# A scaled residual on one core: blocks of 8, 60 and 60 contiguous rows instead of one 128-row block per partition

## The chip, the cores and the metric

The kernel runs on one core of one Trainium2 chip. The metric is the device time in microseconds (us): lower is better. A profile of one execution goes with each kernel. Its span, from the first instruction of the program to the last, is a little shorter than the measured device time.

## The reference

```python
B, S, D = 1024, 16, 512
# x, y: (B, S, D) bfloat16; gamma: (D,) bfloat16
def reference(x, y, gamma):
    return x + gamma * y
```

Seen as a matrix, x and y are 16,384 rows of 512 bfloat16 values, 1 KB a row. The kernel has to read x and y (33.55 MB) and write the result (16.78 MB): 50.33 MB with two arithmetic operations per element.

## The kernel before

Each of the 128 partitions of the on-chip memory (SBUF) gets 128 consecutive rows, so that neighbouring partitions read from places 128 KiB apart in HBM. `SP` and `ACT` list the transfers that the sequencers of SyncE and ScalarE issue, in order, each on a DMA ring of its own: `('y', 4, 64)` loads rows 4 to 64 of every partition, `('x', 64, 117, 0)` does so for x into the buffer rows from 0 on, `('g',)` loads gamma, `('s', 0, 64)` stores. `EARLY` says how many of them are moved ahead of the start-up barrier of the engines.

```python
PIECES = [53, 11, 53, 11]
SP = [('y', 0, 4), ('y', 4, 64), ('x', 0, 64, 0), ('y', 64, 128), ('x', 64, 117, 0), ('x', 117, 128, 64)]
ACT = [('g',), ('s', 0, 64), ('s', 64, 128)]
EARLY = (2, 0)
RELEASE = ('x', 64, 117, 0)
DVE = [('m', 0), ('m', 1), ('a', 0), ('a', 1), ('m', 2), ('m', 3), ('a', 2), ('a', 3)]
# ... (cut)
    xv = xf.rearrange("(p n) d -> p n d", p=P)        # P = 128; the same for yv and ov
# ... (cut)
    y_sb = nc.alloc_sbuf_tensor("y_sb", [P, rows, D], dt).ap()
    x_rows = max(w[3] + w[2] - w[1] for w in x_loads)
    x_sb = nc.alloc_sbuf_tensor("x_sb", [P, x_rows, D], dt).ap()
```

y lies whole in SBUF (128 rows a partition) and the result overwrites it. x has a buffer of 75 rows, parts of which are used twice: a load into rows still in use waits (`frees`) until the additions that read them are done. A store waits for the additions of its rows, and the first one also for `s_go`.

VectorE works through `DVE`: `('m', c)` multiplies piece c of y by gamma, in place, and `('a', c)` adds x to it. `PIECES` has the rows of each piece.

```python
    _take(s_load[RELEASE], 16, nc.tensor)   # when the transfer RELEASE has landed ...
    nc.tensor.sem_inc(s_go, 1)              # ... the stores may start
    nc.tensor.sem_inc(s_rel, 1)
# ... (cut)
    for kind, *args in DVE:
        c = args[0]
        yt = y_sb[:, starts[c] : starts[c + 1], :]
        if kind == "m":
            need(y_loads, c)                # wait for the loads of these rows
            g = gamma_sb[:, None, :].to_broadcast([P, PIECES[c], D])
            nc.vector.tensor_tensor(out=yt, in0=yt, in1=g, op=MULT).then_inc(s_dve, 1)
        else:
            need(x_loads, c)
            # ... (cut)
            nc.vector.tensor_tensor(out=yt, in0=xt, in1=yt, op=ADD).then_inc(s_add, 1)
```

gamma itself is one row; a matmul with a row of ones spreads it over the 128 partitions, and VectorE copies it from there to SBUF.

Of the kernel before, what the change touches and what calls it, by code (L numbers as in the profile page):

```python
# [3 lines left out]


PIECES = [53, 11, 53, 11]

SP = [('y', 0, 4), ('y', 4, 64), ('x', 0, 64, 0), ('y', 64, 128), ('x', 64, 117, 0), ('x', 117, 128, 64)]  # L10
ACT = [('g',), ('s', 0, 64), ('s', 64, 128)]

EARLY = (2, 0)


RELEASE = ('x', 64, 117, 0)

DVE = [('m', 0), ('m', 1), ('a', 0), ('a', 1), ('m', 2), ('m', 3), ('a', 2), ('a', 3)]
MULT, ADD = mybir.AluOpType.mult, mybir.AluOpType.add


def _take(sem, n, eng):


    return eng.wait_ge(sem, n).then_inc(sem, -n)  # L25


def kernel(
# [10 lines left out]
    P = nc.NUM_PARTITIONS  # L39
# [3 lines left out]
    xf = x.flatten_outer_dims()  # L43
    yf = y.flatten_outer_dims()
    of = out.flatten_outer_dims()
    N, D = xf.shape
    rows = N // P
    n = len(PIECES)
    assert sum(PIECES) == rows
    starts = [sum(PIECES[:c]) for c in range(n + 1)]  # L50
    dt = xf.dtype
    xv = xf.rearrange("(p n) d -> p n d", p=P)
    yv = yf.rearrange("(p n) d -> p n d", p=P)
    ov = of.rearrange("(p n) d -> p n d", p=P)

    gamma_row = nc.alloc_sbuf_tensor("gamma_row", [1, D], dt).ap()
    ones_row = nc.alloc_sbuf_tensor("ones_row", [1, P], dt).ap()
# [1 line left out]
    y_sb = nc.alloc_sbuf_tensor("y_sb", [P, rows, D], dt).ap()  # L59
    x_loads = [w for w in SP + ACT if w[0] == "x"]  # L60
    y_loads = [w for w in SP + ACT if w[0] == "y"]
    stores = [w for w in SP + ACT if w[0] == "s"]
    for loads in (x_loads, y_loads, stores):
# [7 lines left out]
    s_load = {w: sem("s_" + "_".join(map(str, w[:2]))) for w in x_loads + y_loads}  # L71
    s_add, s_go, s_rel, s_end, s_out = sem("s_add"), sem("s_go"), sem("s_rel"), sem("s_end"), sem("s_out")
    added = [a for kind, *a in DVE if kind == "a"]
    order = {a[0]: k for k, a in enumerate(added)}

    def meets(a, b, c, d):
        return a < d and c < b

    def pieces_of(a, b):
        return [c for c in range(n) if meets(starts[c], starts[c + 1], a, b)]  # L80

    def x_at(row):
        return next(w[3] + row - w[1] for w in x_loads if w[1] <= row < w[2])

    def frees(w):

        c = set()
        for v in x_loads[: x_loads.index(w)]:
            lo, hi = max(v[3], w[3]), min(v[3] + v[2] - v[1], w[3] + w[2] - w[1])
            if lo < hi:  # L90
                c |= set(pieces_of(v[1] + lo - v[3], v[1] + hi - v[3]))
        return sorted(c)
# [3 lines left out]
    def ring(eng, what, n_early):  # L96

        known, went = 0, False
        for k, w in enumerate(what):
            kind = w[0]  # L100
            need = frees(w) if kind == "x" else pieces_of(w[1], w[2]) + list(w[3:]) if kind == "s" else []
            need = max((order[c] + 1 for c in need), default=0)
            if kind == "s" and not went:
                _take(s_go, 1, eng)
                went = True
            if need > known:
                eng.wait_ge(s_add, need)
                known = need
            if kind == "g":
                i = eng.dma_start(out=gamma_row, in_=gamma.unsqueeze(0)).then_inc(s_gamma, 16)  # L110
            elif kind == "x":
                to = x_sb[:, w[3] : w[3] + w[2] - w[1], :]
                i = eng.dma_start(out=to, in_=xv[:, w[1] : w[2], :]).then_inc(s_load[w], 16)
            elif kind == "y":
                r = slice(w[1], w[2])
                i = eng.dma_start(out=y_sb[:, r, :], in_=yv[:, r, :]).then_inc(s_load[w], 16)
            else:
                r = slice(w[1], w[2])
                i = eng.dma_start(out=ov[:, r, :], in_=y_sb[:, r, :]).then_inc(s_out, 16)
            if k < n_early:  # L120
                early.append(i.ins)

    ring(nc.sync, SP, EARLY[0])
    ring(nc.scalar, ACT, EARLY[1])


# [7 lines left out]

    _take(s_load[RELEASE], 16, nc.tensor)
    nc.tensor.sem_inc(s_go, 1)
# [4 lines left out]
    def need(loads, c):  # L141
        for w in loads:
            if w not in landed and meets(starts[c], starts[c + 1], w[1], w[2]):
                if w == RELEASE:
                    _take(s_rel, 1, nc.vector)
                else:
                    _take(s_load[w], 16, nc.vector)
                landed.add(w)
# [5 lines that stand above are left out]
            need(y_loads, c)  # L154
            g = gamma_sb[:, None, :].to_broadcast([P, PIECES[c], D])
            nc.vector.tensor_tensor(out=yt, in0=yt, in1=g, op=MULT).then_inc(s_dve, 1)  # L156
            open_mults += 1
        else:
# [4 lines left out]
            at = x_at(starts[c])  # L163
            xt = x_sb[:, at : at + PIECES[c], :]
            nc.vector.tensor_tensor(out=yt, in0=xt, in1=yt, op=ADD).then_inc(s_add, 1)  # L165
# [44 lines left out]
```

## Time and profile before

| | before |
|---|---|
| device time, median of 3 runs | 119.94 us (119.78 to 120.6) |
| span of the profiled execution | 118.7 us |
| VectorE busy | 70.0 us, 59% of the span |
| TensorE matmul busy | 0.6 us |
| DMA, both rings | 50.33 MB in 1154 packets, mean 424 GB/s |

How to read it: the page gives the busy time of each engine and cuts the span into 40 slices, in each of which a digit is the busy share in tenths. A DMA transfer is cut into packets, here one for each partition, that 16 DMA engines work on. The queue called q1 is SyncE's ring and q10 ScalarE's. A packet is booked where it starts, so that a slice or a window with a row of long packets starting in it can show more than the engines' whole time, and the next one nothing. A DMA issue is listed with its size and the time from issue to landing, which includes the time that it stood behind others.

### The profile page before, as it was taken

The numbers are of one execution on the slowest core, as the hardware profiler recorded it, in microseconds if no ns is written. First come the engines' busy times: TensorE is split into PE (matmuls) and PEld (weight loads), VectorE is DVE, ScalarE is ACT, GpSimd is POOL, SyncE is SP. The second block draws the span as 40 slices with busy tenths as digits, with TensorE's granted clock in tenths as the row PEclk, the third lists the DMA queues.
The fourth block names the chain that finished last, engine by engine and source line by source line (L and its number), as shares of the span: only waits on it lengthen the run. The fifth ranks groups of instructions, "written<-read, shape, count | busy, mean of one in ns | idle before, by whom it ended". The sixth has DMA issues, their size and how long they took to land. (4 is left out here: it accounts for less than half of the span.)

```text
span 118.7 us, 80 instructions
## 1 busy us (share of the span) xinstructions
PE 0.6 (0%) x1; PEld 0.1 (0%) x1; DVE 70.0 (59%) x10; POOL 0.2 (0%) x4
## 2 busy tenths in 40 slices
PE   0001000000000000000000000000000000000000
PEld 0000000000000000000000000000000000000000
DVE  0002000599999299999759999999999910000000
POOL 0000000000000000000000000000000000000000
DMA  8977977998899888998896969498899889988891
GB/s 268 571 332 331 663 331 331 596 464 353 353 486 574 353 353 353 640 420 353 353 585 293 585 293 585 205 634 353 353 596 464 353 353 420 640 353 353 353 663 44
DMA packets 1154, 50.33 MB, mean 424 GB/s; under 512 B 129, under 2 KB 130, under 8 KB 258
## 3 DMA queue, kind: packets, MB, share of 16 engines
q1 hardware_dynamic: 864, 33.55, 66.0%
q10 hardware_dynamic: 290, 16.78, 32.6%
HBM read 33.56 MB, written 16.78 MB: 424 GB/s over the span
## 5 line engine op out<-in xcount | busy, mean ns | idle before, releaser
L156 DVE TENSOR_TENSOR y_sb<-y_sb,gamma_sb 128x27136 bf16<-128x27136 bf16 (+1 forms) x4 | 34.6, 8688 | 12.3 <-DVEq L25 12.3
L165 DVE TENSOR_TENSOR y_sb<-x_sb,y_sb 128x27136 bf16<-128x27136 bf16 (+1 forms) x4 | 34.6, 8689 | 2.3 <-DVEq L25 2.2
L132 DVE CAST gamma_sb<-gamma_ps 128x512 bf16<-128x512 f32 x1 | 0.7, 692 | 8.8 <-DVEq L25 8.8
L127 DVE MEMSET ones_row<- 1x128 bf16 x1 | 0.2, 165 | 2.0 <-PEq L41 2.0
L130 PE MATMUL gamma_ps<-gamma_row,ones_row 1*128 1x512 bf16 x1 | 0.6, 577 | 10.2 <-PEq L25 10.2
L130 PEld LDWEIGHTS gamma_ps<-gamma_row,ones_row 1*128 1x128 bf16 x1 | 0.1, 99 | 10.2 <-issue 10.2
L194 POOL MEMSET const-bfloat16-1.0<- 128x1 bf16 x1 | 0.1, 101 | 0.0
L194 POOL MEMSET const-uint8-127<- 128x1 uint8 x1 | 0.1, 101 | 0.0
L194 POOL MEMSET const-float32-0.0<- 128x1 f32 x1 | 0.1, 98 | 0.2 <-issue 0.2
L194 POOL MEMSET const-float32-1.0<- 128x1 f32 x1 | 0.1, 98 | 0.0
## 6 DMA issues: line engine op xcount, KB each, us to landing
y_sb<-in_y_dram SPq DMA_DIRECT2D x1, 7680.0 KB, 21.4
x_sb<-in_x_dram SPq DMA_DIRECT2D x1, 6784.0 KB, 20.8
x_sb<-in_x_dram SPq DMA_DIRECT2D x1, 1408.0 KB, 23.8
y_sb<-in_y_dram SPq DMA_DIRECT2D x1, 512.0 KB, 3.8
out_dram<-y_sb ACTq DMA_DIRECT2D x2, 22.8
x_sb<-in_x_dram SPq DMA_DIRECT2D x1, 39.3
gamma_row<-in_gamma_dram ACTq DMA_DIRECT2D x1, 1.0 KB
y_sb<-in_y_dram SPq DMA_DIRECT2D x1, 58.3
```

What stands on the lines that cost most here:

```text
L127: nc.vector.memset(ones_row, 1.0).then_inc(s_ones, 1)
L130: nc.tensor.matmul(gamma_ps, ones_row, gamma_row, start=True, stop=True).then_inc(s_ps, 1)
L132: nc.vector.tensor_copy(out=gamma_sb, in_=gamma_ps).then_inc(s_dve, 1)
L156: nc.vector.tensor_tensor(out=yt, in0=yt, in1=g, op=MULT).then_inc(s_dve, 1)
L165: nc.vector.tensor_tensor(out=yt, in0=xt, in1=yt, op=ADD).then_inc(s_add, 1)
L194: nc = _bacc.Bacc("TRN2", target_bir_lowering=False, num_devices=1)
```

## The change

The rows are cut into three blocks, the first with 8 rows for each partition and the other two with 60; within a block the rows of all partitions lie together in HBM, so that a partition's 8 (or 60) rows are next to those of its neighbours. The first 8 rows of y come as two transfers of 4 rows, one on each ring, both ahead of the start-up barrier. The first 8 rows of x are loaded last of all loads, behind the transfer that releases the stores, and their result is stored last. The pieces and the order of VectorE's work follow from this: in the middle block the last 45 rows are added first, since the next load of x overwrites their place.

The aim is that the first transfers set all DMA engines to work at once, on addresses that lie close together, that small pieces stand at the start and at the end of the work, and that x's 8 rows keep the engines busy between the release of the stores and their first packets.

```diff
-PIECES = [53, 11, 53, 11]
-SP = [('y', 0, 4), ('y', 4, 64), ('x', 0, 64, 0), ('y', 64, 128), ('x', 64, 117, 0), ('x', 117, 128, 64)]
-ACT = [('g',), ('s', 0, 64), ('s', 64, 128)]
-EARLY = (2, 0)
-RELEASE = ('x', 64, 117, 0)
-DVE = [('m', 0), ('m', 1), ('a', 0), ('a', 1), ('m', 2), ('m', 3), ('a', 2), ('a', 3)]
+BLOCKS = [8, 60, 60]
+PIECES = [8, 15, 45, 60]
+SP = [
+    ('y', 0, 4),
+    ('y', 8, 68),
+    ('x', 8, 68, 0),
+    ('y', 68, 128),
+    ('x', 68, 128, 15),
+    ('x', 0, 8, 0),
+]
+ACT = [('y', 4, 8), ('g',), ('s', 8, 68), ('s', 68, 128), ('s', 0, 8)]
+EARLY = (2, 1)
+RELEASE = ('x', 68, 128, 15)
+DVE = [('m', 0), ('m', 1), ('m', 2), ('a', 2), ('a', 1), ('m', 3), ('a', 3), ('a', 0)]
...
-    xv = xf.rearrange("(p n) d -> p n d", p=P)
...
+    def rows_of(t, a, b):
+        c = max(c for c in range(len(BLOCKS)) if edges[c] <= a)
+        assert b <= edges[c + 1]
+        block = t[P * edges[c] : P * edges[c + 1]].rearrange("(p n) d -> p n d", p=P)
+        return block[:, a - edges[c] : b - edges[c], :]
...
-                i = eng.dma_start(out=to, in_=xv[:, w[1] : w[2], :]).then_inc(s_load[w], 16)
+                i = eng.dma_start(out=to, in_=rows_of(xf, w[1], w[2])).then_inc(s_load[w], 16)
```

(The loads of y and the stores are changed in the same way.)

More of the change, by code (lines that the diff above doesn't have):

```diff
@@ L51 @@
     dt = xf.dtype
-    xv = xf.rearrange("(p n) d -> p n d", p=P)
-    yv = yf.rearrange("(p n) d -> p n d", p=P)
-    ov = of.rearrange("(p n) d -> p n d", p=P)
+    edges = [sum(BLOCKS[:c]) for c in range(len(BLOCKS) + 1)]
+    assert edges[-1] == rows
+    def rows_of(t, a, b):
[3 more added lines that the diff above has]
+        return block[:, a - edges[c] : b - edges[c], :]
     gamma_row = nc.alloc_sbuf_tensor("gamma_row", [1, D], dt).ap()
@@ L112, in ring @@
                 to = x_sb[:, w[3] : w[3] + w[2] - w[1], :]
-                i = eng.dma_start(out=to, in_=xv[:, w[1] : w[2], :]).then_inc(s_load[w], 16)
+                i = eng.dma_start(out=to, in_=rows_of(xf, w[1], w[2])).then_inc(s_load[w], 16)
             elif kind == "y":
                 r = slice(w[1], w[2])
-                i = eng.dma_start(out=y_sb[:, r, :], in_=yv[:, r, :]).then_inc(s_load[w], 16)
+                i = eng.dma_start(out=y_sb[:, r, :], in_=rows_of(yf, w[1], w[2])).then_inc(s_load[w], 16)
             else:
                 r = slice(w[1], w[2])
-                i = eng.dma_start(out=ov[:, r, :], in_=y_sb[:, r, :]).then_inc(s_out, 16)
+                i = eng.dma_start(out=rows_of(of, w[1], w[2]), in_=y_sb[:, r, :]).then_inc(s_out, 16)
             if k < n_early:
```

## The prediction

> **What bounds the kernel now.** I read the page first (busy shares, then the slices, then the queues), then the DMA view for sizes and landings, then the timeline and the waits of VectorE, and last the DMA view of narrow windows, to get the time of one packet. The page:
>
> ```profile
> DVE  0002000599999299999759999999999910000000
> ...
> DMA  8977977998899888998896969498899889988891
> ...
> DMA packets 1154, 50.33 MB, mean 424 GB/s; under 512 B 129, under 2 KB 130, under 8 KB 258
> ## 3 DMA queue, kind: packets, MB, share of 16 engines
> q1 hardware_dynamic: 864, 33.55, 66.0%
> q10 hardware_dynamic: 290, 16.78, 32.6%
> ```
>
> Together the two queues keep the 16 DMA engines busy for 66.0 + 32.6 = 98.6% of the 118.7 us span, or 117.0 us per engine; VectorE has 70.0 us in all and ends at 95.4 us. So this is a kernel that moves 50.33 MB and hides everything else. The chain of waits is of little use here: it names 10.4% of "issue" and one VectorE add, because what is waited for is a transfer.
>
> The DMA view of four short windows gives the time of a packet (16 packets, one per engine, start in the last two; the share is their whole duration over 16 engines x the window). Windows 1.0 to 1.5, 2.0 to 2.5, 5 to 6 and 115 to 116 us:
>
> ```profile
> q1 hardware_dynamic: 16, 0.07, 138.4%
> ...
> q1 hardware_dynamic: 46, 0.19, 98.6%
> ...
> q1 hardware_dynamic: 16, 0.98, 226.7%
> ...
> q10 hardware_dynamic: 16, 1.05, 241.8%
> ```
>
> - 5 to 6 us: 60-row packets, 61,440 B each, 2.267 us. That is 27.1 GB/s per engine, 434 GB/s for 16.
> - 115 to 116 us: the stores' 65,536 B packets take 2.418 us, the same rate. They are the last; the span ends at 118.7.
> - 1.0 to 1.5 us: the first 16 packets of 4,096 B. 138.4% x 16 x 0.5 / 16 = 0.69 us each.
> - 2.0 to 2.5 us: the same kind of packet takes 0.986 x 16 x 0.5 / 46 = 0.17 us (0.159 in nearly all single records).
>
> So only the start is slow. The window 1.4 to 2.0 us has 17 packet starts, where 16 engines at 0.159 us could start 60. After that no engine stands still: the landings of the loads, issue time plus time to landing, follow at the packet rate. The lines for them and the timeline of VectorE:
>
> ```profile
> y_sb<-in_y_dram SPq DMA_DIRECT2D x1, 7680.0 KB, 21.4
> x_sb<-in_x_dram SPq DMA_DIRECT2D x1, 6784.0 KB, 20.8
> x_sb<-in_x_dram SPq DMA_DIRECT2D x1, 1408.0 KB, 23.8
> y_sb<-in_y_dram SPq DMA_DIRECT2D x1, 512.0 KB, 3.8
> ...
> y_sb<-in_y_dram SPq DMA_DIRECT2D x1, 58.3
> ```
>
> ```profile
> 10.97 0.69 DVE L132 CAST gamma_sb<-gamma_ps 128x512 bf16<-128x512 f32 x1 [8.81 <-DVEq L25]
> 21.99 17.29 DVE L156 TENSOR_TENSOR y_sb<-y_sb,gamma_sb 128x27136 bf16<-128x27136 bf16 x2 [10.33 <-DVEq L25]
> 41.46 17.29 DVE L165 TENSOR_TENSOR y_sb<-x_sb,y_sb 128x27136 bf16<-128x27136 bf16 x2 [2.17 <-DVEq L25]
> 60.69 17.29 DVE L156 TENSOR_TENSOR y_sb<-y_sb,gamma_sb 128x27136 bf16<-128x27136 bf16 x2 [1.94 <-DVEq L25]
> 78.13 17.30 DVE L165 TENSOR_TENSOR y_sb<-x_sb,y_sb 128x27136 bf16<-128x27136 bf16 x2
> ```
>
> y's first 4 rows land at 3.8 us, its next 60 at 21.9 (18.1 later; 8 packets x 2.267 = 18.1), x's 64 at 41.2, y's 64 at 60.6, x's 53 at 76.6 and 11 at 79.9; the second store is issued at 95.5, some 3 us before the engines have finished the first.
>
> **What the Trainium skill says.** "DMA: Bandwidth & Descriptors", section "Where 436 GB/s comes from", gives a ceiling of 435.2 GB/s; the 434 above agrees, so no layout in HBM can speed up the steady part. Its section "Latency and other measured facts" lists row pitches of 512 KiB (207 GB/s per direction) to 8 MiB (103) for HBM copies, the large ones slow. Here the pitch between partitions is 128 rows x 1 KB = 128 KiB and the rate is full, so there is nothing of that to mend in mid-stream. Its section "Queues, rings and completion order" says that each engine goes round robin between queues by packet. The trace shows what it means for a small transfer: gamma, issued at 1.91 us on ScalarE's ring, has its 1 KB packet only in the window 7 to 8 us and its semaphore packet in 9 to 10, between 61,440 B packets of the other ring. "Issuing engines are not separate DMA queues" says that a second ring saves issue time alone.
>
> **The change part by part.** Everything is worked per engine, because each has a fixed 8 of the 128 partitions and 8 packets of every transfer, and the slowest sets the end.
>
> 1. *Bytes:* the same 50.33 MB. At 61,440 B per 2.267 us, 3.146 MB per engine are 116.1 us, in both kernels.
> 2. *Packets.* 8 packets x durations. Before: 0.159 (4 rows) + 2.267 (60) + 2.418 x 2 (x and y 64) + 2.004 (53) + 0.422 (11) + 2.418 x 2 (stores) = 14.52, x 8 = 116.2 us. After: 0.159 x 2 + 2.267 x 4 loads + 2.267 x 2 stores + 0.310 x 2 (x's 8 rows in and out) = 14.54, x 8 = 116.3. The 0.310 is an estimate from 0.159 at 4 KB and 0.422 at 11 KB. The smaller packets cost 0.1 us.
> 3. *Start.* Packet work of 116.2 in a span of 118.7 leaves 2.5 us: 1.0 from issue to the first packet, about 0.35 from the last engine's last packet to the end (semaphores), and about 1.1 of ramp and spread between engines. The ramp is the 0.69 against 0.159 us of the first packet (0.5), then the empty stretch until the second (a few tenths). The change works on this in two ways. The second ring puts another 4 KB packet in front of each engine in that stretch: at most one or two packets of 0.159 us, 0.15 to 0.3. The rows of 1 MB in one block, instead of 128 places 128 KiB apart, may shorten the first access; nothing in this trace shows it, so I count 0 to 0.3.
> 4. *VectorE.* It is as busy as before: 14.291 us / 53 rows = 0.270 us a row, so 256 row-steps are 69 us. Expected order: y's 8 rows landed by about 5 us, gamma somewhere at 8 to 15 (now behind y's 4 rows on its ring), multiply of 8 rows 2.2 us, done before y 8:68 lands at about 22.9. Multiplies of 15 and 45 rows until 39.2; x 8:68 lands at 41.1; add of 45 rows until 53.4, add of 15 until 57.5. Multiply of 60: 59.3 to 75.6; x 68:128 lands at 77.3; add of 60 until 93.6; add of 8 until 95.8.
> 5. *Reloads.* x 68:128 needs only the 45-row add, so it is issued at 53.4 instead of 55.8; the engines run out of y at about 58.9 (landing 59.3 less 0.35). Issue to first packet took 1.0 at the start, so 4 us are spare. x's 8 rows wait until 57.5, with 18 us of x 68:128 still ahead of them.
> 6. *Stores.* Released by x 68:128 at 77.3 + 0.35. From there to packets was at most 2 us before. x's 8 rows now cover 8 x 0.31 = 2.5 us of it where 11 rows covered 3.4. The fastest engine may stand still for a tenth or two; the slowest is 0.6 behind and does not. Second store: issued at 93.6, engines busy with the first until about 97.5. Third at 95.8, queued far ahead.
>
> Sum: +0.1 for packets, -0.2 to -0.5 for the ramp, 0 for the rest: about -0.3 us. 119.94 - 0.3 = 119.6 us. The unit of the gain is the ramp, and all of it is 1.1 us, 0.9%.
>
> **The rivals.**
> - *The rings start at different moments.* If ScalarE's 4 rows come behind even a few of SyncE's 4 KB packets, the leftover ones each wait out a 2.267 us packet, as gamma did: y's rows 4 to 8 then land at 10 to 20 us and gamma after them. The bytes still flow, and VectorE has until about 22.9 - 2.2 = 20.7. For it: gamma's delay; against: ScalarE's first instruction in this trace is at 0.13 us, as early as SyncE's. Time unchanged to +0.3 only if gamma passes 25 us, as the slack behind it is 2 us at x 8:68 and 4 at the reload.
> - *A gap at the turn from loads to stores,* if 2.5 us of cover are too few. Against it: in the trace the stores' first packets follow the 11-row packets on every engine without a gap. If the store's lead is really above 2.5 us: +0.2 to +0.6, 120.2.
> - *Contiguity is worth more than I count.* If the ramp vanishes and the engines finish together: -1.0, 118.9. A full rate of 434 in mid-stream forbids more.
> - *Spread:* the end is the slowest engine's; 0.64 us lie between the first and the last engine's final packet in the window 117.6 to 118.7. With two rings it may shrink or grow by some tenths.
>
> **Range and chances.** The terms have a width of about 0.4 us each way and the three runs before spread from 119.78 to 120.6; hence 119.6, with 119.1 to 120.2 for 8 in 10. Two per cent is 2.4 us. A gain of that size would need the whole ramp and a rate above the ceiling; a loss of that size needs a hole in the transfers that none of the slacks (4 us and 4 us) suggests. So 0.02 faster, 0.95 within 2%, 0.03 slower.
>
> **What would show it.** Right: 16-packet windows of 2.267 us throughout, a queue share still at 98 to 99%, the first x reload issued near 53.4, the first store near 77.6, and the 60-row packets starting before 4.3 us on all engines (y's 1 MB at full rate needs 2.6 from 1.0, plus ramp). Step 3 is wrong if the first packets of both rings take the same 0.7 us with the same empty stretch, step 6 if slices near 78 to 80 us fall under the mean. All of it is wrong if packets of the new layout take longer than 2.267 us.

## The result, and the profile after

The changed kernel takes 120.75 us (median of 5 runs, 120.69 to 120.8) against 119.89 us (119.78 to 120.6): 1.0067 times the time before, with a 95% interval of 1.0047 to 1.0088. It is slower by 0.7%, and outside the predicted range. The spans of the two profiled executions differ by 0.7 us (119.4 and 118.7).

The page of the changed kernel: the slices and the queues.

```profile
DVE  0004500099999489999589999559999950000000
...
DMA  5999889979979979979989989697997997897796
...
DMA packets 1442, 50.33 MB, mean 421 GB/s; under 512 B 161, under 2 KB 162, under 8 KB 418
## 3 DMA queue, kind: packets, MB, share of 16 engines
q1 hardware_dynamic: 864, 33.03, 64.6%
q10 hardware_dynamic: 578, 17.30, 33.6%
```

The bytes are the same and the engines are as busy as before, 64.6 + 33.6 = 98.2% of the span. The one slice that stands out is the first, the first 3 us: 5 tenths, where the page before has 8. The DMA view of the window 12 to 20 us shows that the 60-row packets are as they were:

```profile
q1 hardware_dynamic: 49, 3.01, 86.8%
```

86.8% x 16 x 8 us / 49 packets = 2.267 us, to the last digit the time of a 61,440 B packet before. So it is the start. The same view in the windows 1.0 to 1.5, 1.5 to 2.0, 2.0 to 2.5 and 2.5 to 3.0 us (in the last one, two queues):

```profile
q1 hardware_dynamic: 21, 0.09, 53.9%
...
q1 hardware_dynamic: 29, 0.12, 84.0%
...
q1 hardware_dynamic: 29, 0.12, 99.7%
...
q1 hardware_dynamic: 21, 0.09, 82.1%
q10 hardware_dynamic: 7, 0.03, 13.9%
```

These are 4 KB packets. In the first window they take 53.9% x 8 us / 21 = 0.21 us each, where the kernel before needed 0.69: the first access did get shorter. But then they get slower, 84.0% x 8 / 29 = 0.23, 99.7% x 8 / 29 = 0.275 and 82.1% x 8 / 21 = 0.31 us, where the kernel before had 0.17 at 2.0 to 2.5 us, 46 packets in half a microsecond instead of 29. And engines stand empty: the packets of the first window fill at most 53.9% of the engines' time. In the packet records of the trace (start, duration and size of every packet) eight packets are under way from 1.3 to 1.7 us, for 16 engines; the kernel before has 14. The change was to set all engines to work at once, and here did the opposite. ScalarE's ring, q10, has no packet at all until the last of these windows; its first one starts at 2.77 us. Its packets take 0.159 us.

The packet records give the sum. The slowest engine starts its first 60-row packet at 5.255 us (before: 3.384). That is 1.87 later, and 8 more packets of 0.159 explain 1.27; 0.60 us are lost. From there to the last packet of the slowest engine it is 118.979 - 5.255 = 113.72 us (before: 118.336 - 3.384 = 114.95), 1.23 less; since 1.27 of the work has moved ahead, 0.04 is lost. The end after the last packet has 0.45 instead of 0.37 us. 0.60 + 0.04 + 0.08 = 0.72, the difference of the spans. The further 0.14 us between the two device times is in no view; other executions of the kernel before with a span of 118.7 us took about 120.0 us, so that most of it is spread between executions.

What the 0.60 us consist of can be worked out too. Per engine, the 4 KB packets ahead of the 60-row ones take 0.72 us more than 0.159 each (before: 0.64, of which 0.53 in the first). From 1.0 us to its first 60-row packet, an engine is without a packet for 0.44 us (before: 0.18). And the slowest engine is 0.55 us behind the mean (before: 0.29): eight engines start their first 60-row packet at 4.29 to 4.45 us, the other eight at 4.94 to 5.26. So longer packets alone give 0.08 of the 0.60, because the shorter first access pays for most of them; gaps and unevenness give 0.26 each.

The timeline after, for the order of the rest:

```profile
0.00 0.84 SPq L130 DMA_DIRECT2D y_sb<-in_y_dram  x2
0.12 0.38 ACTq L130 DMA_DIRECT2D y_sb<-in_y_dram  x1
...
54.40 4.40 SPq L127 DMA_DIRECT2D x_sb<-in_x_dram  x2
60.24 16.16 DVE L170 TENSOR_TENSOR y_sb<-y_sb,gamma_sb 128x30720 bf16<-128x30720 bf16 x1 [1.80 <-DVEq L33]
78.60 19.02 ACTq L133 DMA_DIRECT2D out_dram<-y_sb  x3
78.89 18.36 DVE L179 TENSOR_TENSOR y_sb<-x_sb,y_sb 128x30720 bf16<-128x30720 bf16 x2 [2.49 <-DVEq L33]
```

The second ring's transfer is issued 0.12 us after the first, so the late q10 packets are not a late issue. Reloads and stores are issued in the expected order, each 0.9 to 1.5 us later than expected, and VectorE still waits for the transfers.

### The profile page after: what moved, and what is told of

It is laid out like the page before. It is cut to its first block, busy times and chain, and to the rows that moved or that the text cites. A ratio compares the mean times of both kernels' runs of the same rounds, so it can differ in the third digit from the quotient of the medians.

```text
span 119.4 us, 83 instructions
## 1 busy us (share of the span) xinstructions
PE 0.6 (0%) x1; PEld 0.1 (0%) x1; DVE 70.1 (59%) x10; POOL 0.2 (0%) x4
## 3 DMA queue, kind: packets, MB, share of 16 engines
q1 hardware_dynamic: 864, 33.03, 64.6%
q10 hardware_dynamic: 578, 17.30, 33.6%
## 5 line engine op out<-in xcount | busy, mean ns | idle before, releaser
L170 DVE TENSOR_TENSOR y_sb<-y_sb,gamma_sb 128x4096 bf16<-128x4096 bf16 (+3 forms) x4 | 34.7, 8690 | 12.6 <-DVEq L33 12.6
L179 DVE TENSOR_TENSOR y_sb<-x_sb,y_sb 128x23040 bf16<-128x23040 bf16 (+3 forms) x4 | 34.6, 8686 | 4.5 <-DVEq L33 4.5
```

## The experiments

Each kernel was timed beside the kernel before on the same chip, so that the ratios compare the groups and the times do so only roughly; that one had medians of 120.02, 120.05, 120.02 and 120.06 us in the four groups below. "Start loss" is worked out from the packet records: the start of the slowest engine's first packet of 60 (in one run 64) rows, less the 1.0 us to the first packet and the packets ahead of it at 0.159 us for 4 KB (16 or 8 of them) or 0.309 us for 8 KB (8 of them). The kernel before has 3.38 - 1.0 - 1.27 = 1.11 us, the changed one 5.255 - 1.0 - 2.544 = 1.71. It is that of the one profiled execution; those of e6_pitch16 (121.02 us) and e12_pitch32 (120.41) were 0.2 and 0.4 us above their medians.

### First group: the ring, the layout, the number of packets

```diff
 # e1_one_ring, against the changed kernel
-    ('y', 0, 4), ('y', 8, 68),
+    ('y', 0, 4), ('y', 4, 8), ('y', 8, 68),
-ACT = [('y', 4, 8), ('g',), ...
+ACT = [('g',), ...
-EARLY = (2, 1)
+EARLY = (3, 0)
 # e2_wide_two_rings
-BLOCKS = [8, 60, 60]
+BLOCKS = [128]
 # e3_wide_one_ring: both of the above
 # e4_one_transfer
-    ('y', 0, 4), ('y', 8, 68),
+    ('y', 0, 8), ('y', 8, 68),
-ACT = [('y', 4, 8), ('g',), ...
+ACT = [('g',), ...
-EARLY = (2, 1)
+EARLY = (2, 0)
```

> The changed kernel, but all of y's first 8 rows on SyncE's ring: two transfers of 4 rows, one behind the other, then the 60 rows. Theory A (the contiguous addresses of the first rows slow its 4 KB packets, 0.248 us on average against 0.159): the ring does not matter, 120.7 us, the slowest engine still starts its 60-row packets near 5.2 us. Theory B (the second ring is what slows the start: two transfers are set up side by side): back to about 120.0 us, 60-row packets from 4.6 us at the latest. Theory C (16 small packets per engine at the start instead of 8 cost it, wherever they come from): 120.7 us.

> The changed kernel with its order and both rings, but the rows laid out as before, 128 consecutive rows a partition. Theory A: the 4 KB packets of the start take 0.16 us again after their first, about 119.9 to 120.1 us. Theory B: 120.7 us. Theory C: 120.7 us.

> Layout of before and one ring for y's first rows, with the pieces and the order of the changed kernel. Theory A: as with two rings in this layout, 119.9 to 120.1 us. Theory B: 120.0 us. Theory C: still 120.7 us, as the 16 small packets are there. If all of it comes from the start, this one is within 0.2 us of the kernel before under A and B.

> The changed kernel with y's first 8 rows as one transfer of 8 KB packets on SyncE's ring. Theory A: the packets are contiguous over the whole 1 MB, still slow for a start of the same length: 120.4 to 120.7 us. Theory B: 120.0 us. Theory C: half of the small packets are gone, 120.2 us.

| kernel | us | ratio to before (95%) | start loss, us |
|---|---|---|---|
| e1_one_ring | 120.79 | 1.0065 (1.0053 to 1.0077) | 1.76 |
| e2_wide_two_rings | 120.04 | 1.0001 (0.9994 to 1.0009) | 1.08 |
| e3_wide_one_ring | 120.1 | 1.0005 (0.9997 to 1.0013) | 1.08 |
| e4_one_transfer | 119.87 | 0.9989 (0.9981 to 0.9996) | 0.86 |

The ring does nothing in either layout, so theory B falls. The layout does everything, with all 16 small packets in place: theory C falls too. The DMA view of e2_wide_two_rings, 2.0 to 2.5 us, has the line of before again, 46 packets at 1.012 x 8 / 46 = 0.18 us:

```profile
q1 hardware_dynamic: 46, 0.19, 101.2%
```

Theory A had the three first runs right and missed the fourth: one 8 KB transfer of the same 1 MB is fast. In its view from 1.5 to 2.5 us 40 packets of 8 KB start, 0.33 MB where the changed kernel has 0.24 MB in 58:

```profile
q1 hardware_dynamic: 40, 0.33, 81.7%
```

So it is not that the rows lie close together. What differs between the two, besides the size and number of the packets, is that a 4-row transfer takes 4 KB and leaves out the next 4 KB, through the whole block. In the packet records it has eight packets under way until 1.55 us, like the changed kernel, but then all engines start their 60-row packets within 0.25 us: eight engines that start late are not a loss by themselves. This kernel is also a little faster than both kernels of the case.

### Second group: the distance between the places that are read, and the second ring's late start

```diff
 # e5_pitch4, e6_pitch16: y's two first transfers alone
-    in_=rows_of(yf, w[1], w[2])
+    in_=src
 #  e5:  src = yf[128 * w[1] : 128 * w[2]].rearrange("(p n) d -> p n d", p=P)
 #  e6:  src = yf[0 : 16 * P].rearrange("(p n) d -> p n d", p=P)[:, r, :]
 # e7_scalar_first
-EARLY = (2, 1)
+EARLY = (0, 1)
 # e8_before_no_small, against the kernel before
-SP = [('y', 0, 4), ('y', 4, 64), ('x', 0, 64, 0), ...
+SP = [('y', 0, 64), ('x', 0, 64, 0), ...
-EARLY = (2, 0)
+EARLY = (1, 0)
```

In e5 and e6 (and in e12 to e14 below), y's first 8 rows of each partition are other rows of y than the reference asks for; the work is the same.

> The changed kernel, but y's first two transfers read 4 KB a partition from places 4 KB apart: each is one closed block of 512 KB. Other rows of y than the reference wants come to these places; bytes, packets, rings and order are those of the changed kernel. Theory A1 (a transfer that takes 4 KB and leaves 4 KB out, over 1 MB, uses only a part of what serves these addresses): the 4 KB packets are back to 0.16 us, the time near 120.1 us. Theory A2 (4 KB packets from any small stretch of HBM are slow, since all 16 engines read it at once): as slow or slower, 120.7 us or more, packets of 0.25 us or more.

> As the run before, with places 16 KB apart: 4 KB read, 12 KB left out, over 2 MB. A1: a quarter of these addresses is used at a time, slower than the changed kernel, 121 us or more, packets of 0.4 us. A2: a longer stretch is better, 120.2 to 120.6 us. With places 128 KB apart the packets took 0.159 us, so if this one is fast too, only the 8 KB pitch is bad.

> The changed kernel, with SyncE's two first transfers put back behind the start-up barrier, so that ScalarE's 4 rows of y are the only early transfer. In the changed kernel ScalarE issues them at 0.12 us and their first packet starts at 2.77. Theory S (transfers of both rings are set up one after the other): here the first packet comes 1.0 us after the issue. Theory L (ScalarE's ring is slow to begin): again 2.5 us or more after the issue.

> The kernel before, with y's rows 0 to 64 as one first transfer instead of 4 and 60 rows. If small packets at the start only add their 0.008 us each and the slow first access is paid once whatever its size, 119.8 to 119.95 us, as with one 8 KB transfer in the changed kernel. If a small first transfer does something for the start, 120.2 us or more.

| kernel | us | ratio to before (95%) | start loss, us |
|---|---|---|---|
| e5_pitch4 | 119.78 | 0.9981 (0.9974 to 0.9988) | 0.76 |
| e6_pitch16 | 120.81 | 1.0065 (1.0049 to 1.008) | 1.89 |
| e7_scalar_first | 122.49 (one run) | | |
| e8_before_no_small | 119.98 | 0.9996 (0.9987 to 1.0004) | |

e5_pitch4 is the sharpest run of all: against the changed kernel nothing is different but 4 KB from every 4 KB instead of 4 KB from every 8 (and so which rows come), and 0.97 us are gone. It is the two-ring start as it was meant to be. Its DMA view from 1.5 to 2.5 us, both queues:

```profile
q1 hardware_dynamic: 89, 0.36, 97.8%
q10 hardware_dynamic: 3, 0.01, 5.2%
```

92 packets at 1.03 x 16 / 92 = 0.18 us, against 58 at 0.25 us in the changed kernel, whose line for this window is

```profile
q1 hardware_dynamic: 58, 0.24, 91.9%
```

Theory A2 falls. A1 has e5 right in kind (it said 120.1), but not e6: with a quarter in use the loss is barely larger than with a half, 1.89 us against 1.71, and the packets do not take 0.4 us on average. The same view of e6_pitch16, 0.863 x 16 / 45 = 0.31 us:

```profile
q1 hardware_dynamic: 45, 0.18, 86.3%
```

e7_scalar_first answers for the ring. Its timeline and the window 1.0 to 1.5 us:

```profile
0.13 0.38 ACTq L130 DMA_DIRECT2D y_sb<-in_y_dram  x1
```

```profile
q10 hardware_dynamic: 15, 0.06, 35.5%
```

Alone, ScalarE's transfer has its first packet at 1.14 us, 1.01 after the issue; behind SyncE's it took 2.65. So ScalarE's ring is not slow to begin, and theory L falls. Theory S fits: the second ring's packets came late because the first ring's were ahead of them (in the changed kernel 91 of SyncE's 128 had started by 2.77 us), and could not fill the empty moment after the first packets. How the transfers are set up is in no trace. (The time of 122.49 us only says that a late start on SyncE costs what it delays.) The run shows something else as well: SyncE's rows 0 to 4, here the second transfer over the same block, are slow too. In the window 3.5 to 4.5 us, where 60 of the 63 packets are of 4 KB and the others write semaphores, 0.972 x 16 / 60 = 0.26 us:

```profile
q1 hardware_dynamic: 63, 0.25, 97.2%
```

e8_before_no_small lies just above its forecast of 119.8 to 119.95 and is not distinguishable from the kernel before: leaving out the small first transfer neither helps nor hurts.

### Third group: elsewhere in the work, versions that are right for the reference, and 32 KB

```diff
 # e9_split_late, against e4_one_transfer
-    ('x', 0, 8, 0),
+    ('x', 0, 4, 0), ('x', 4, 8, 4),
 # e10_two_closed, against the changed kernel
-BLOCKS = [8, 60, 60]
+BLOCKS = [4, 4, 60, 60]
-    ('x', 0, 8, 0),                 # and ('s', 0, 8)
+    ('x', 0, 4, 0), ('x', 4, 8, 4), # and ('s', 0, 4), ('s', 4, 8)
 # e11_one_closed4
+BLOCKS = [4, 64, 60]
+PIECES = [4, 15, 49, 60]
+SP = [('y', 0, 4), ('y', 4, 68), ('x', 4, 68, 0), ('y', 68, 128),
+      ('x', 68, 122, 15), ('x', 122, 128, 69), ('x', 0, 4, 0)]
+ACT = [('g',), ('s', 4, 68), ('s', 68, 128), ('s', 0, 4)]
+EARLY = (2, 0)
+RELEASE = ('x', 68, 122, 15)
 # e12_pitch32: as e6_pitch16, with 32 in place of 16
```

> The kernel with y's 8 rows as one transfer (119.87 us), in which x's 8 rows now come as two transfers of 4 rows, 4 KB read and 4 KB left out, in the middle of the work. Theory P (the half-used stretch is slow wherever it stands in the work): these packets take 0.25 us and the slowest engine loses 0.6, about 120.4 us. Theory W (only at the start, where nothing of these addresses was touched and the queues are empty): packets of 0.159 us, 119.9 to 120.0 us.

> The changed kernel with its first block cut into two blocks of 4 rows, so that each of y's two first transfers reads a closed 512 KB, and every row goes where the reference wants it; x's and the result's 8 rows come in two transfers each. Theory A1: 4 KB packets of 0.159 us after the first; 119.8 to 119.95 us, since the four more 4-row transfers cost about 0.1 us against the same start with 8-row transfers (119.78).

> Blocks of 4, 64 and 60 rows: a single closed 4-row transfer of y first, on SyncE's ring; the stores released by x's rows 68 to 122, with 6 and 4 rows of x behind them. Fewest small packets with a closed start: A1 expects 119.65 to 119.8 us, faster than the kernel before (120.0) and than the changed one. If the gain of the closed start needs two rings, 119.9 us.

> The changed kernel with y's first 4-row transfers reading 4 KB from places 32 KB apart (other rows of y than the reference wants). Places 8 and 16 KB apart gave 120.7 to 120.8, 4 KB 119.78 and 128 KB 120.04. If what counts is the share of a stretch that is used, 120.8 or more; if it is the length of the stretch (4 MB here), between 120.0 and 120.5 us.

| kernel | us | ratio to before (95%) | start loss, us |
|---|---|---|---|
| e9_split_late | 120.37 | 1.0028 (1.0017 to 1.004) | 0.95 |
| e10_two_closed | 119.86 | 0.9991 (0.9983 to 0.9999) | 0.74 |
| e11_one_closed4 | 119.94 | 0.9988 (0.9981 to 0.9994) | 0.60 |
| e12_pitch32 | 120.02 | 0.9999 (0.999 to 1.0008) | 1.15 |

e9_split_late shows that the pattern is slow in mid-stream too. x's 4-row transfer, in the middle of a busy ring, from 77.2 to 77.7 us:

```profile
q1 hardware_dynamic: 39, 0.16, 120.0%
```

1.2 x 8 / 39 = 0.25 us for 4 KB. In the kernel without the split (e4_one_transfer, 77.5 to 78.0 us) 8 KB take 1.044 x 8 / 27 = 0.31:

```profile
q1 hardware_dynamic: 27, 0.22, 104.4%
```

The split costs 120.37 - 119.87 = 0.5 us. In the packet records the loss is in the first of the two 4-row transfers, whose packets reach 0.40 us; the second transfer of x takes 0.159 us in all of them. It is not the splitting as such: e10_two_closed has two 4-row transfers of x in the same place, each from a closed block, and their 256 packets take 0.159 us on average and none over 0.17. Why the second pass over such a block is fast here and in the changed kernel, but not in e7_scalar_first, remains open.

e10_two_closed and e11_one_closed4 compute what the reference asks for and, like e4_one_transfer, are faster than the kernel before by about 0.1%, with intervals that just exclude 1; with so many runs side by side that is weak. e11 missed its forecast of 119.65 to 119.8: it starts best of all (0.60), but the first 64-row packets behind it take up to 2.68 us instead of 2.42, so a part of the loss may have moved on to them. e12_pitch32 contradicts the reading that only the share counts: an eighth of 4 MB is in use, and it is as fast as 128 KB. Its forecast for a reading by the length of the stretch, 120.0 to 120.5 us, is met. Its line for 1.5 to 2.5 us, 0.736 x 16 / 68 = 0.17 us:

```profile
q1 hardware_dynamic: 68, 0.28, 73.6%
```

### Fourth group: powers of two, or any part

```diff
 # e13_pitch12, e14_pitch24: as e6_pitch16, with 12 and 24 in place of 16
```

> The changed kernel with y's first 4-row transfers reading 4 KB from places 12 KB apart (other rows of y than the reference wants). Theory U (any small stretch that is used in part is slow): a third of 1.5 MB is used at a time, between 8 KB (120.7) and 16 KB (120.8), so 120.7 us. Theory Z (only distances that are powers of two, 8 and 16 KB, make the 16 engines meet; the odd multiple 3 x 4 KB does not): 119.8 to 120.1 us, and the packets at 1.5 to 2.5 us take 0.16 to 0.18.

> As the run before, with places 24 KB apart, 3 x 8 KB, over 3 MB. Theory U, with the stretch beginning to be long enough (32 KB apart gave 120.02): 120.2 to 120.6 us. Theory Z: 24 KB is a multiple of 8 KB, but not a power of two; 119.8 to 120.1 us, or, if the factor of 8 KB is what counts, as slow as 8 KB, 120.7.

| places apart | 4 KB | 8 KB | 12 KB | 16 KB | 24 KB | 32 KB | 128 KB |
|---|---|---|---|---|---|---|---|
| us | 119.78 | 120.75 | 120.13 | 120.81 | 120.41 | 120.02 | 120.04 |
| start loss, us | 0.76 | 1.71 | 1.13 | 1.89 | 1.44 | 1.15 | 1.08 |
| of it: packets over 0.159 | 0.20 | 0.72 | 0.72 | 0.64 | 0.69 | 0.49 | 0.62 |
| engine without a packet | 0.26 | 0.44 | 0.15 | 0.59 | 0.25 | 0.28 | 0.13 |
| slowest engine behind the mean | 0.29 | 0.55 | 0.27 | 0.67 | 0.49 | 0.38 | 0.33 |

The 8 KB column is the changed kernel, the 128 KB column e2_wide_two_rings, where all transfers have this distance; in the others only y's two first ones have the distance named. The three parts are worked out from the packet records, per engine and up to the first 60-row packet, and rounded.

e13_pitch12 is at 1.0013 (1.0006 to 1.002) and e14_pitch24 at 1.0037 (1.0023 to 1.0052). The window 1.5 to 2.5 us of e13_pitch12, 0.631 x 16 / 53 = 0.19 us:

```profile
q1 hardware_dynamic: 53, 0.22, 63.1%
```

That of e14_pitch24, 0.726 x 16 / 47 = 0.25 us:

```profile
q1 hardware_dynamic: 47, 0.19, 72.6%
```

12 KB uses less of its stretch than 8 KB and is fast, so theory U falls: being used in part is not enough. (Its forecast for 24 KB, 120.2 to 120.6 us, was met, but by an allowance for the length of the stretch.) Theory Z comes close at 12 KB (120.13 against its 119.8 to 120.1; 0.19 against 0.16 to 0.18 us), but at 24 KB it offered either a fast start or one as slow as 8 KB, and the run lies between. So 4 and 12 KB are fast, 8 and 16 KB slow, 24 KB half as bad, 32 and 128 KB fast. That looks like engines meeting at the same places of the memory, by the distance of what they read at the same time; this is argued from the pattern, not shown, and no run here looks at the memory itself.

The parts in the table warn against a simpler story. At 12 and 128 KB the packets together take as long as at 8 and 16 KB: their first ones are slow (0.65 and 0.63 us on average for the first 16), the later ones fast. What 8 and 16 KB have more of is time without a packet and distance between the engines. Only at 4 KB are the packets themselves clearly shorter.

## Why the prediction was wrong, by its own steps

**The bound, and step 1 (bytes):** right. The engines stay 98% busy and the 60-row packets take 2.267 us.

**Step 2 (packets):** right. It put +0.1 us on the smaller packets. In the packet records all packets take 117.24 us per engine instead of 117.01; without the 0.07 of it at the start, 0.16 more.

**Step 3 (start): here it failed**, in both of its terms; the 1.1 us that it put on ramp and spread before are confirmed (1.11). "The second ring puts another 4 KB packet in front of each engine in that stretch": the second ring's first packet started at 2.77 us, when that stretch was over, behind the first ring's (alone it comes 1.01 us after its issue, e7_scalar_first); and taking the ring away changes nothing (e1_one_ring, e3_wide_one_ring). The stretch was also narrower than the step read it. Few packets start in it because the first ones last up to 1.16 us; up to its first 60-row packet an engine of the kernel before is without one for 0.18 us on average.

The contiguous block "may shorten the first access; nothing in this trace shows it, so I count 0 to 0.3": it did shorten it, 0.21 us against 0.69 in the first half microsecond, but the packets after it took longer, which all but used this up (0.72 us over 0.159 each instead of 0.64). Gaps and unevenness came on top, so that the start lost 0.60 us where 0.2 to 0.5 was to be gained. The error was to take contiguity as something that can only help. In the changed kernel y's two first transfers are not contiguous: the block is, but each of them reads every other 4 KB of it, a distance of 8 KB that the trace before had no example of. 128 KB had been seen to be harmless, and the step took for granted that a smaller distance is no worse. e5_pitch4 shows what the step had in mind: with really closed transfers the same kernel takes 119.78 us. The range failed with it, as it left nothing for a worse start. Of the signs that the prediction named, one told: the 60-row packets were to start before 4.3 us on all engines, and start at 4.29 to 5.26.

**Steps 4 to 6:** right in order, 0.9 to 1.5 us late in every time, which fits a start that lost 0.60 us and engines that are further apart. The reload was issued at 54.40 us (53.4 expected), VectorE ended at 97.2 (95.8), the first store was issued at 78.60 (77.65). The turn from loads to stores went as written: in the packet records the fastest engines stand still for 0.1 to 0.3 us, the slowest for nothing.

**The rivals:** late rows and a late gamma did not come (y's rows 4 to 8 landed at 5.6 us, and gamma let the matmul start at 9.4 us, earlier than before). The gap at the turn had no weight. "Contiguity is worth more than I count" had the wrong sign, and no rival said that it could cost something. "Spread" pointed at the right place, the distance between the engines at the start, without a cause or the size: they now start their 60-row packets over 0.97 us (4.29 to 5.26) instead of 0.60.

**What the prediction cited:** The Trainium skill's page "DMA: Bandwidth & Descriptors", section "Latency and other measured facts", lists distances between rows from 512 KiB up, with a rate that falls as they grow. In this case 128 KiB was fine and 8 and 16 KB were not; the prediction read a list of large distances as if small ones were safe. What it took from the section "Issuing engines are not separate DMA queues", that a second ring saves issue time alone, was the better guide, and step 3 went against it: e1_one_ring and e3_wide_one_ring agree with the page.

## What to carry to other kernels

When a layout is made contiguous, look at what each single transfer reads: two halves of a row block are two strided transfers. With 8 or 16 KB between 4 KB pieces, y's first transfers lost 1.71 and 1.89 us at the start, against 0.76 with closed ones: their packets took 40 to 70% longer at 1.5 to 2.5 us (0.25 and 0.31 us against 0.18), and the engines had more gaps and drifted apart. For 8 KB the longer packets were there in mid-stream too. One 8 KB transfer, or two blocks that are each closed, avoid it. In a kernel whose DMA engines are busy for 98%, a small loss at the start is carried to the end (0.60 of the 0.72 us here), so the packets of narrow windows say more than the shares of the page. A mean packet time is not enough: count also how many packets are under way, and how far apart the engines are.

## What the runs showed of the hardware that had not been expected

- At 1.5 to 2.5 us, 4 KB packets from places 8, 16 or 24 KB apart took 0.25 to 0.31 us on average, from places 4, 12 or 32 KB apart 0.17 to 0.19, and 0.159 in the steady state.
- In the changed kernel eight packets were under way from 1.3 to 1.7 us, and at the turn to the stores, near 79.4 us, eight engines were still 0.7 us ahead of the other eight on average.
- Of two such passes over one block, the second ran at 0.159 us in the changed kernel and in mid-stream (e9_split_late), but at 0.26 us for a stretch in e7_scalar_first.
- A transfer issued on ScalarE's ring 0.12 us after one on SyncE's had its first packet 2.65 us after its issue; alone it took 1.01 us.
